# A dense layer with squared ReLU on one core: a new order of the first loads, and shared transposes for the tail columns of x

## The chip, the cores and the metric

The kernel runs on one core of a Trainium2 chip. The metric is the device time of one execution in microseconds; before the change three executions gave 290.81, 291.29 and 291.22, median 291.22. The profiled execution took 290.52, of which the profile's span is 288.7.

## What is computed

x is 2048 rows of D = 576 in bf16, w1 is 576 x 4608, w2 is 4608 x 576:

```python
h = jnp.einsum("bsd,df->bsf", x, w1) + b1
r = jnp.where(h > zero, h, zero)
h = r * r
out = jnp.einsum("bsf,fd->bsd", h, w2) + b2
```

576 is four and a half times 128. The half, the last 64 columns of x and the last 64 rows of w1, is what makes the layout below uneven.

## The kernel before, in words

The rows are worked in four token blocks of 512 (SB). For each block the kernel needs x transposed, with the 576 contraction values on the partitions. For blocks 1 to 3 the DMA transposes on the way in (load_xT). For block 0, x is loaded as it lies (load_x, line 71, four tiles of 128 rows, 144 KB each) and turned on TensorE, against an identity matrix, into PSUM, and copied from there to SBUF.

The transposed block, xT, has nine windows of 512 columns on 128 partitions, since the kernel uses TensorE in two ways. The first four of 36 feature tiles (G = 4) are computed with full 128-row matmuls: four chunks of 128 contraction rows, w1n, and a last 64-row piece, w1n8, for which two tiles go side by side, one on the upper and one on the lower 64 rows of the array (pair, lines 195 to 199). The other 32 feature tiles are computed in a row-split loop (a_rows, line 172): nine chunks of 64 rows each, one feature tile on partitions 0 to 63 and one on 64 to 127 at the same time. For this each half needs chunks that the transposes put on the other half, so two copies (dup_windows, line 113) duplicate four windows from one half of the partitions to the other. In names: windows O to O+3 are the four full chunks, E3 and SPC hold the tail and its neighbour, E to E+2 the shifted ones.

Each feature tile's PSUM bank is emptied by ScalarE (relu with bias, line 169) and squared by VectorE (line 170). After two blocks, phase_t and phase_b multiply by w2 and add b2, and then the other two blocks follow.

The order of the work is written by hand: keep() holds instructions in program order on each engine, and every engine works through its own stream. Loads are issued from SyncE and from ScalarE, each of which has a queue of its own. A load that reuses one of the eight completion semaphores waits until the earlier transfer on it has landed.

The head of the kernel, which the change concerns, is this:

- Seven matmuls on constants (WARM, line 61) keep TensorE busy until x arrives.
- SyncE issues x tiles 0 and 2, w1n chunks 0 and 2, the two halves of w1n8, and then the weights of the row-split loop (line 82). ScalarE issues x tiles 1 and 3 and w1n chunks 1 and 3, then loads its activation table with a small activation (line 97), and then issues b1 (line 98).
- Each x tile takes five transposes (x_transpose, line 141): four full chunks and the last 128 columns (D - P to D). So the tail transpose covers 64 columns that are in chunk 3 already. After two tiles the PSUM banks are copied (x_copies, line 148), by VectorE for three windows and by ScalarE for two. dup_windows(0) comes after the second half.
- The first four feature tiles are then summed chunk by chunk over half blocks of 256 columns (part(h, k), line 214), with the bias's transpose (make_b1T, line 157) in between, and finished by the pairs.

Of the kernel before, what the change touches and what calls it, by code (L numbers as in the profile page):

```python
# [9 lines left out]
ACT = mybir.ActivationFunctionType  # L10
ALU = mybir.AluOpType
BF16 = mybir.dt.bfloat16
FP32 = mybir.dt.float32
# [4 lines left out]
def kernel(  # L18
# [9 lines left out]
    nc = tc.nc  # L28
    keep = tc.keep_in_program_order
    P = 128  # L30
    H = 64
    x2 = x.flatten_outer_dims()
    out2 = out.flatten_outer_dims()
    S, D = x2.shape
    F = w1.shape[1]
    NFT = F // P
    NC = D // H
    NK = NC // 2
# [6 lines left out]
    RT = SB // P  # L45
# [3 lines left out]
    const = ctx.enter_context(tc.tile_pool(name="const", bufs=1))  # L49
# [6 lines left out]
    ps_h = ctx.enter_context(tc.tile_pool(name="ps_h", bufs=4, space=PSUM))  # L56
# [1 line left out]

    wps = ps_h.tile([P, 512], FP32, name="wps", tag="ph")
    ones = nc.const_aps.tensor(1.0, [P, 512], BF16)  # L60
    WARM = [512] * 6 + [256]
    for i, n in enumerate(WARM):
        keep(nc.tensor.matmul(wps[:, 0:n], lhsT=ones[:, 0:P], rhs=ones[:, 0:n], start=True, stop=True))  # L63

    xs = const.tile([P, RT, D], BF16, name="x_sb")
    w1n = wpool.tile([P, NK, GW], BF16, name="w1n")
# [4 lines left out]
    def load_x(eng, rt):  # L71
        keep(eng.dma_start(out=xs[:, rt, :], in_=x2[rt * P:(rt + 1) * P, :]))  # L72

    def load_w1n(eng, k0, k1):
        src = w1[k0 * P:k1 * P, 0:GW].rearrange("(k p) f -> p k f", p=P)
        keep(eng.dma_start(out=w1n[:, k0:k1, :], in_=src))

    def load_w1n8(eng, h):
        keep(eng.dma_start(out=w1n8[h * H:(h + 1) * H, :], in_=w1[NK * P:D, 0:GW]))
# [5 lines left out]
    b1_rows = const.tile([P, P], BF16, name="b1_rows")  # L85
    nc.vector.memset(b1_rows[:], 0.0)
    load_x(nc.sync, 0)
    load_x(nc.scalar, 1)
    load_x(nc.sync, 2)
    load_x(nc.scalar, 3)  # L90
    for k in range(NK):
        load_w1n(nc.sync if k % 2 == 0 else nc.scalar, k, k + 1)

    ident = const.tile([P, P], BF16, name="ident")
    make_identity(nc, ident[:])
    warm = const.tile([P, 1], FP32, name="warm")
    keep(nc.scalar.activation(out=warm[:], in_=nc.const_aps.tensor(0.0, [P, 1], FP32), func=ACT.Relu))
    keep(nc.scalar.dma_start(out=b1_rows[0:NFT, :], in_=b1.rearrange("(ft p) -> ft p", p=P)))
    for h in range(2):
        load_w1n8(nc.sync, h)  # L100

    E3, O, SPC, E = 0, 1, 5, 6
    LO_W = [O, O + 1, O + 2, O + 3, E, E + 1, E + 2, E3, SPC]
# [9 lines left out]
    def dup_windows(sb):  # L113
        xT = xT_blk[sb]
        keep(nc.vector.tensor_copy(out=xT[0:H, SPC:SPC + 4, :], in_=xT[H:P, E3:E3 + 4, :]))  # L115
        keep(nc.vector.tensor_copy(out=xT[H:P, SPC:SPC + 4, :], in_=xT[0:H, O:O + 4, :]))  # L116
# [18 lines left out]
    xT0 = xT_blk[0]  # L135
    HS = SB // 2
    tb = [[ps_h.tile([P, 4, HS], BF16, name="tb", tag="ph") for _ in range(2)] for _ in range(2)]
    PLACE = [(0, 0), (0, 1), (1, 0), (1, 1), (0, 2)]
    T_ORDER = [0, 1, NK, 2, 3]

    def x_transpose(j):
        h, q = divmod(j, 2)
        for k in T_ORDER:
            bank, slot = PLACE[k]
            c0 = k * P if k < NK else D - P
            keep(nc.tensor.transpose(tb[h][bank][:, slot, q * P:(q + 1) * P], xs[:, j, c0:c0 + P], ident[:]))

    def x_copies(h):
        hc = slice(h * HS, (h + 1) * HS)
        for k in (0, 1):  # L150
            keep(nc.vector.tensor_copy(out=xT0[:, O + k, hc], in_=tb[h][0][:, k, :]))
        keep(nc.scalar.copy(out=xT0[:, O + 2:O + 4, hc], in_=tb[h][1][:, 0:2, :]))  # L152
        keep(nc.vector.tensor_copy(out=xT0[:, E3, hc], in_=tb[h][0][:, 2, :]))

    b1T = const.tile([P, NFT], FP32, name="b1T")

    def make_b1T():
        b1T_ps = ps_h.tile([P, P], BF16, name="b1T_ps", tag="ph")
        keep(nc.tensor.transpose(b1T_ps[:], b1_rows[:], ident[:]))  # L159
        keep(nc.vector.tensor_copy(out=b1T[:], in_=b1T_ps[:, 0:NFT]))  # L160
# [6 lines left out]
    def evac_h(sb, bank, ft):  # L167
        r = rpool.tile([P, SB], BF16, name="r", tag="r")
        keep(nc.scalar.activation(out=r[:], in_=bank[:], func=ACT.Relu, bias=b1T[:, ft:ft + 1], scale=1.0))  # L169
        keep(nc.vector.tensor_tensor(out=hTs[sb][:, ft, :], in0=r[:], in1=r[:], op=ALU.mult))  # L170
# [17 lines left out]
    def a_full(sb, order):  # L188
        xT = xT_blk[sb]
        banks = []  # L190
        for g in range(G):
            pool, tag = (ps_o, "po") if g < 2 or order == "k_outer" else (ps_h, "ph")
            banks.append(pool.tile([P, SB], FP32, name="pn", tag=tag))

        def pair(i, start, stop):
            keep(nc.tensor.matmul(banks[2 * i][:], lhsT=w1n8[0:H, 2 * i * P:(2 * i + 1) * P], rhs=xT[0:H, SPC, :],  # L196
                             start=start, stop=stop, skip_group_check=order == "k_outer"))
            keep(nc.tensor.matmul(banks[2 * i + 1][:], lhsT=w1n8[H:P, (2 * i + 1) * P:(2 * i + 2) * P], rhs=xT[H:P, E3, :],  # L198
                             start=start, stop=stop, skip_group_check=order == "k_outer"))

        def full(g, k, start, stop):
            keep(nc.tensor.matmul(banks[g][:], lhsT=w1n[:, k, g * P:(g + 1) * P], rhs=xT[:, O + k, :],  # L202
                             start=start, stop=stop))

        if order == "rows_first":
            for i in (1, 0):
                pair(i, True, False)
            for g in (2, 3, 0, 1):
                for k in range(NK):
                    full(g, k, False, k == NK - 1)  # L210
                evac_h(sb, banks[g], g)
        else:
            if order == "k_outer":
                def part(h, k):
                    hc = slice(h * HS, (h + 1) * HS)
                    for g in range(G):
                        keep(nc.tensor.matmul(banks[g][:, hc], lhsT=w1n[:, k, g * P:(g + 1) * P],  # L217
                                              rhs=xT[:, O + k, hc], start=(h == 0 and k == 0), stop=False,
                                              skip_group_check=True))

                for j in range(2):
                    x_transpose(j)
                x_copies(0)
                for j in range(2, RT):
                    x_transpose(j)
                x_copies(1)
                dup_windows(0)
                for k in range(NK):
                    part(0, k)
                part(1, 0)  # L230
                make_b1T()
                for k in range(1, NK):
                    part(1, k)
            else:
                for g in (2, 3, 0, 1):
                    for k in range(NK):
                        full(g, k, k == 0, False)
            for i in (1, 0):
                pair(i, False, True)
                evac_h(sb, banks[2 * i], 2 * i)  # L240
                evac_h(sb, banks[2 * i + 1], 2 * i + 1)
# [42 lines left out]
    b2_col = const.tile([P, 1], BF16, name="b2_col")  # L284
    keep(nc.sync.dma_start(out=b2_col[:], in_=b2[DM:D].rearrange("(d o) -> d o", o=1)))
    b2T = const.tile([P, 1], FP32, name="b2T")
    nc.gpsimd.tensor_copy(out=b2T[:], in_=b2_col[:])
    keep(nc.sync.dma_start(out=b2_bc[:], in_=b2.partition_broadcast(P)))
    for c in range(2):
        load_w2(c)  # L290
# [1 line left out]

    alloc_hT(0)
    a_full(0, "k_outer")
    a_rows(0, 12, 1)
    alloc_hT(1)
    load_xT(3)
    a_rows(1)
    a_full(1, "rows_first")
    phase_t(0, hTs[0])  # L300
    phase_t(1, hTs[1])
    phase_b(0, hTs[0], dups=(2, 3))
    phase_b(1, hTs[1])
    alloc_hT(2)
    a_full(2, "g_outer")
    a_rows(2)
    alloc_hT(3)
# [36 lines left out]
```

## Time and profile before

| what | number |
|---|---|
| median of three executions | 291.22 us |
| span of the profile | 288.7 us |
| TensorE busy | 284.6 us, 99% |
| ScalarE, VectorE busy | 96.5, 78.6 us |
| row-split matmuls, lines 181 and 183 | 576 each, mean 376 ns |
| part, line 217 | 32 matmuls of 256 columns, first at 5.4 us |
| first pair, line 196 | 9.06 us |
| activation table load, line 97 | 1283 ns, at 2.61 us |

A busy TensorE in this profile is not a TensorE at its peak: matmuls are pipelined and their ends are modelled, so the start of one to the start of the next is the time that counts. The instructive part is the head: of its transfers the profile gives the issue and the time from issue to landing (x 2.8 to 3.2 us, w1n 3.5 to 3.9, w1n8 2.5 to 2.8).

### The profile page before, as it was taken

The numbers are of one execution on the slowest core, as the hardware profiler recorded it, in microseconds if no ns is written. First come the engines' busy times: TensorE is split into PE (matmuls) and PEld (weight loads), VectorE is DVE, ScalarE is ACT, GpSimd is POOL, SyncE is SP. The second block draws the span as 40 slices with busy tenths as digits, with TensorE's granted clock in tenths as the row PEclk, the third lists the DMA queues.
The fourth block names the chain that finished last, engine by engine and source line by source line (L and its number), as shares of the span: only waits on it lengthen the run. The fifth ranks groups of instructions, "written<-read, shape, count | busy, mean of one in ns | idle before, by whom it ended". The sixth has DMA issues, their size and how long they took to land.

```text
span 288.7 us, 4690 instructions
## 1 busy us (share of the span) xinstructions
PE 284.6 (99%) x2027; PEld 138.9 (48%) x2032; DVE 78.6 (27%) x177; ACT 96.5 (33%) x152; POOL 0.9 (0%) x7
## 2 busy tenths in 40 slices
PE   8999999999999999999999999999999999999996
PEld 5544444444444555555544444444444455555555
DVE  3444544444500200000025444444440001100001
ACT  3666666666500000000027666666670000000000
POOL 0000000000000000000000000000000000000000
PEclk9999999999999999999999999999999999999999
DMA  6999999600001100000000000000000110000000
GB/s 198 236 244 197 265 388 246 94 0 2 0 18 36 37 16 18 16 16 18 16 16 2 1 2 0 2 0 2 0 2 0 36 39 16 16 16 19 32 17 18
DMA packets 31573, 16.59 MB, mean 57 GB/s; under 512 B 15552, under 2 KB 31552, under 8 KB 31552
## 3 DMA queue, kind: packets, MB, share of 16 engines
q1 hardware_dynamic: 30928, 15.72, 22.3%
q10 hardware_dynamic: 624, 0.57, 0.7%
q8 instruction: 16, 0.26, 0.4%
q14 instruction: 5, 0.04, 0.0%
HBM read 11.43 MB, written 2.36 MB: 48 GB/s over the span
## 4 chain that ended last, share of the span: by engine, by line
PE 97%; DMA 1%; SPq 0%; issue 0%; DVE 0%
PE ph L181 42%; PE po L272 38%; PE pt L253 11%; PE pn L202 4%; DMA w1n<-in_w_dram 1%; PE pn L217 1%; PE ph L183 1%; PE pn L196 1%; SPq L72 0%; DVE o_sb L274 0%; PE b1T_ps L159 0%; PE pn L198 0%
## 5 line engine op out<-in xcount | busy, mean ns | idle before, releaser
L181 PE MATMUL ph<-xTw,w_h 64*128 64x512 bf16 x576 | 124.6, 376 | 0.0
L183 PE MATMUL ph<-xTw,w_h 64*128 64x512 bf16 x576 | 124.6, 376 | 0.0
L272 PE MATMUL po<-w_sb,hT 128*128 128x448 bf16 (+2 forms) x612 | 109.4, 341 | 0.0
L169 ACT ACTIVATE r<-ph,b1T 128x512 bf16<-128x512 f32 x128 | 81.1, 685 | 41.6 <-PE ph L183 41.6
L181 PEld LDWEIGHTS <-w_h 64*128 64x128 bf16 x576 | 54.1, 94 | 68.3
L272 PEld LDWEIGHTS <-hT 128*128 128x128 bf16 x612 | 58.5, 98 | 51.0
L170 DVE TENSOR_TENSOR hT<-r 128x512 bf16<-128x512 bf16 x144 | 61.2, 426 | 76.9 <-ACT r L169 76.9
L183 PEld LDWEIGHTS <-w_h 64*128 64x128 bf16 x576 | 54.1, 94 | 0.0
L274 DVE TENSOR_TENSOR o_sb<-po,b_bc 128x448 bf16<-128x448 f32 (+2 forms) x17 | 10.2, 597 | 125.8 <-PE po L272 125.8
L253 PE MATMUL pt<-hT,w_sb 128*128 128x512 bf16 x142 | 31.3, 379 | 0.1
L169 ACT ACTIVATE r<-pn,b1T 128x512 bf16<-128x512 f32 x16 | 10.3, 688 | 62.0 <-PE pn L198 60.6
L253 PEld LDWEIGHTS <-w_sb 128*128 128x128 bf16 x144 | 14.1, 98 | 17.0
L256 ACT ACTIVATE oT<-pt,b2T 128x512 bf16<-128x512 f32 x4 | 2.7, 687 | 28.3 <-PE pt L253 28.3
L202 PE MATMUL pn<-xTw,w1n 128*128 128x512 bf16 x45 | 10.4, 379 | 0.4 <-issue 0.3
L202 PEld LDWEIGHTS <-w1n 128*128 128x128 bf16 x48 | 4.5, 98 | 6.0 <-issue 0.8
L217 PE MATMUL pn<-xTw,w1n 128*128 128x256 bf16 x32 | 3.7, 273 | 0.1
L63 PE MATMUL wps<-const-bfloat16-1.0 128*128 128x512 bf16 (+1 forms) x7 | 2.9, 597 | 0.8 <-PEq L328 0.8
L217 PEld LDWEIGHTS <-w1n 128*128 128x128 bf16 x32 | 3.0, 98 | 0.6 <-DMA w1n<-in_w_dram 0.3
L115 DVE COPY xTw<-xTw 64x2048 bf16<-64x2048 bf16 x4 | 2.8, 690 | 0.6 <-ACT xTw L152 0.5
L116 DVE COPY xTw<-xTw 64x2048 bf16<-64x2048 bf16 x4 | 2.8, 688 | 0.1
L196 PE MATMUL pn<-xTw,w1n 64*128 64x512 bf16 x8 | 2.4, 379 | 0.0
L198 PE MATMUL pn<-xTw,w1n 64*128 64x512 bf16 x8 | 2.4, 379 | 0.0
(21 smaller groups left out, 10.5 us busy)
## 6 DMA issues: line engine op xcount, KB each, us to landing
w_sb<-in_w_dram SPq DMA_DIRECT2D x2, 2592.0 KB, 15.2
w_h<-in_w_dram SPq DMA_DIRECT2D x14, 288.0 KB, 6.6
out_dram<-o_sb SPq DMA_DIRECT2D x15, 112.0 KB, 1.7
w_h<-in_w_dram SPq DMA_DIRECT2D x4, 144.0 KB, 3.2
out_dram<-ot SPq DMA_DIRECT2D x4, 128.0 KB, 2.0
x_sb<-in_x_dram ACTq DMA_DIRECT2D x2, 144.0 KB, 3.0
x_sb<-in_x_dram SPq DMA_DIRECT2D x2, 144.0 KB, 3.0
w1n<-in_w_dram ACTq DMA_DIRECT2D x2, 128.0 KB, 3.6
```

The costliest lines, as they stand in the source:

```text
L63: keep(nc.tensor.matmul(wps[:, 0:n], lhsT=ones[:, 0:P], rhs=ones[:, 0:n], start=True, stop=True))
L115: keep(nc.vector.tensor_copy(out=xT[0:H, SPC:SPC + 4, :], in_=xT[H:P, E3:E3 + 4, :]))
L169: keep(nc.scalar.activation(out=r[:], in_=bank[:], func=ACT.Relu, bias=b1T[:, ft:ft + 1], scale=1.0))
L170: keep(nc.vector.tensor_tensor(out=hTs[sb][:, ft, :], in0=r[:], in1=r[:], op=ALU.mult))
L181: keep(nc.tensor.matmul(bx[:], lhsT=w1_h[0:H, LO_C[i], jc], rhs=xT[0:H, LO_W[i], :], start=(i == 0), stop=(i == NC - 1)))
L183: keep(nc.tensor.matmul(by[:], lhsT=w1_h[H:P, UP_C[i], jc], rhs=xT[H:P, UP_W[i], :], start=(i == 0), stop=(i == NC - 1)))
L196: keep(nc.tensor.matmul(banks[2 * i][:], lhsT=w1n8[0:H, 2 * i * P:(2 * i + 1) * P], rhs=xT[0:H, SPC, :], start=start, stop=stop, skip_grou ...
L202: keep(nc.tensor.matmul(banks[g][:], lhsT=w1n[:, k, g * P:(g + 1) * P], rhs=xT[:, O + k, :], start=start, stop=stop))
L217: keep(nc.tensor.matmul(banks[g][:, hc], lhsT=w1n[:, k, g * P:(g + 1) * P], rhs=xT[:, O + k, hc], start=(h == 0 and k == 0), stop=False, s ...
L253: keep(nc.tensor.matmul(pt[:], lhsT=w2_sb[:, ft, DM:D], rhs=hT[:, ft, :], start=(i == 0), stop=(i == NFT - 1)))
L272: keep(nc.tensor.matmul(po[:, 0:d1 - d0], lhsT=hT[:, ft, jj * P:(jj + 1) * P], rhs=w2_sb[:, ft, d0:d1], start=(i == 0), stop=(i == NFT - 1)))
L274: keep(nc.vector.tensor_tensor(out=o_sb[:, d0:d1], in0=po[:, 0:d1 - d0], in1=b2_bc[:, d0:d1], op=ALU.add))
```

## The change

It reorders the loads of the head. All four x tiles go on SyncE's queue, one after the other. ScalarE starts with the table load, whose small activation now writes one column of w1n chunk 0; the load of that chunk overwrites the column, so it is issued after the activation. Then ScalarE issues b1, chunks 0 and 2, and both halves of w1n8; SyncE has chunks 1 and 3.

The tail columns are no longer transposed with each tile. GpSimd gathers the 64 tail columns of two x tiles side by side (xs8), and one transpose turns both, so four tail transposes become two; they stand between the second and third part. The copies that spread their halves to E3 and SPC, and one shifted copy of four windows, are on VectorE. The shifted copy of three windows to the lower half goes to ScalarE (dup_windows_first). ScalarE copies two windows of the second half block only, where it copied two of each half. The warm-up is 384 columns shorter. The aim is an earlier first tile of x, less work on TensorE before the first matmuls, and less on VectorE.

```diff
-    WARM = [512] * 6 + [256]
+    WARM = [512] * 5 + [384]
...
     load_x(nc.sync, 0)
-    load_x(nc.scalar, 1)
-    load_x(nc.sync, 2)
-    load_x(nc.scalar, 3)
+    keep(nc.scalar.activation(out=w1n[:, 0, 0:1], in_=nc.const_aps.tensor(0.0, [P, 1], FP32), func=ACT.Relu))
+    keep(nc.scalar.dma_start(out=b1_rows[0:NFT, :], in_=b1.rearrange("(ft p) -> ft p", p=P)))
+    for rt in range(1, RT):
+        load_x(nc.sync, rt)
     for k in range(NK):
-        load_w1n(nc.sync if k % 2 == 0 else nc.scalar, k, k + 1)
+        load_w1n(nc.scalar if k % 2 == 0 else nc.sync, k, k + 1)
+    for h in range(2):
+        load_w1n8(nc.scalar, h)
...
-    warm = const.tile([P, 1], FP32, name="warm")
-    keep(nc.scalar.activation(out=warm[:], in_=nc.const_aps.tensor(0.0, [P, 1], FP32), func=ACT.Relu))
-    keep(nc.scalar.dma_start(out=b1_rows[0:NFT, :], in_=b1.rearrange("(ft p) -> ft p", p=P)))
+    xs8 = const.tile([P, RT, H], BF16, name="xs8")
     for h in range(2):
-        load_w1n8(nc.sync, h)
+        keep(nc.gpsimd.tensor_copy(out=xs8[:, 2 * h:2 * h + 2, :], in_=xs[:, 2 * h:2 * h + 2, NK * P:D]))
...
     def x_transpose(j):
         h, q = divmod(j, 2)
-        for k in T_ORDER:
-            bank, slot = PLACE[k]
-            c0 = k * P if k < NK else D - P
-            keep(nc.tensor.transpose(tb[h][bank][:, slot, q * P:(q + 1) * P], xs[:, j, c0:c0 + P], ident[:]))
-
-    def x_copies(h):
         hc = slice(h * HS, (h + 1) * HS)
-        for k in (0, 1):
-            keep(nc.vector.tensor_copy(out=xT0[:, O + k, hc], in_=tb[h][0][:, k, :]))
-        keep(nc.scalar.copy(out=xT0[:, O + 2:O + 4, hc], in_=tb[h][1][:, 0:2, :]))
-        keep(nc.vector.tensor_copy(out=xT0[:, E3, hc], in_=tb[h][0][:, 2, :]))
+        for bank in range(2):
+            for k in range(2 * bank, 2 * bank + 2):
+                keep(nc.tensor.transpose(tb[h][bank][:, k % 2, q * P:(q + 1) * P], xs[:, j, k * P:(k + 1) * P], ident[:]))
+            for k in range(2 * bank, 2 * bank + 2) if q == 1 else ():
+                copy = nc.scalar.copy if h == 1 and bank == 1 else nc.vector.tensor_copy
+                keep(copy(out=xT0[:, O + k, hc], in_=tb[h][bank][:, k % 2, :]))
...
+    def dup_windows_first():
+        keep(nc.scalar.copy(out=xT0[0:H, E:E + 3, :], in_=xT0[H:P, O:O + 3, :]))
+
+    def transpose_tails():
+        tl = ps_h.tile([P, 2, P], BF16, name="tl", tag="ph")
+        for h in range(2):
+            keep(nc.tensor.transpose(tl[:, h, :], xs8[:, 2 * h:2 * h + 2, :], ident[:]))
+        x8 = xT0.rearrange("p c (h q t) -> p c h q t", h=2, q=2)
+        for q in range(2):
+            keep(nc.vector.tensor_copy(out=x8[H:P, E3, :, q, :], in_=tl[q * H:(q + 1) * H, 0:2, :]))
+        for q in range(2):
+            keep(nc.vector.tensor_copy(out=x8[0:H, SPC, :, q, :], in_=tl[q * H:(q + 1) * H, 0:2, :]))
+        keep(nc.vector.tensor_copy(out=xT0[H:P, SPC:SPC + 4, :], in_=xT0[0:H, O:O + 4, :]))
+        keep(nc.vector.tensor_copy(out=xT0[0:H, E3, :], in_=xT0[H:P, O + 3, :]))
...
-                for j in range(2):
+                for j in range(RT):
                     x_transpose(j)
-                x_copies(0)
-                for j in range(2, RT):
-                    x_transpose(j)
-                x_copies(1)
-                dup_windows(0)
+                dup_windows_first()
+                part(0, 0)
+                part(0, 1)
+                transpose_tails()
+                part(0, 2)
+                part(0, 3)
                 for k in range(NK):
-                    part(0, k)
-                part(1, 0)
-                make_b1T()
-                for k in range(1, NK):
                     part(1, k)
+                    if k == 1:
+                        make_b1T()
```

The last edit of the diff fixes the place of a small GpSimd cast (b2T) in that engine's stream.

More of the change, by code (lines that the diff above doesn't have):

```diff
@@ L137 @@
     tb = [[ps_h.tile([P, 4, HS], BF16, name="tb", tag="ph") for _ in range(2)] for _ in range(2)]
-    PLACE = [(0, 0), (0, 1), (1, 0), (1, 1), (0, 2)]
-    T_ORDER = [0, 1, NK, 2, 3]
     def x_transpose(j):
         h, q = divmod(j, 2)
-        for k in T_ORDER:
-            bank, slot = PLACE[k]
-            c0 = k * P if k < NK else D - P
-            keep(nc.tensor.transpose(tb[h][bank][:, slot, q * P:(q + 1) * P], xs[:, j, c0:c0 + P], ident[:]))
-    def x_copies(h):
-        hc = slice(h * HS, (h + 1) * HS)
-        for k in (0, 1):
-            keep(nc.vector.tensor_copy(out=xT0[:, O + k, hc], in_=tb[h][0][:, k, :]))
-        keep(nc.scalar.copy(out=xT0[:, O + 2:O + 4, hc], in_=tb[h][1][:, 0:2, :]))
-        keep(nc.vector.tensor_copy(out=xT0[:, E3, hc], in_=tb[h][0][:, 2, :]))
-    b1T = const.tile([P, NFT], FP32, name="b1T")
+        hc = slice(h * HS, (h + 1) * HS)
+        for bank in range(2):
[4 more added lines that the diff above has]
+                keep(copy(out=xT0[:, O + k, hc], in_=tb[h][bank][:, k % 2, :]))
+    b1T = const.tile([P, NFT], FP32, name="b1T")
+    def dup_windows_first():
[11 more added lines that the diff above has]
+        keep(nc.vector.tensor_copy(out=xT0[0:H, E3, :], in_=xT0[H:P, O + 3, :]))
     def make_b1T():
@@ L286 @@
     b2T = const.tile([P, 1], FP32, name="b2T")
-    nc.gpsimd.tensor_copy(out=b2T[:], in_=b2_col[:])
+    keep(nc.gpsimd.tensor_copy(out=b2T[:], in_=b2_col[:]))
     keep(nc.sync.dma_start(out=b2_bc[:], in_=b2.partition_broadcast(P)))
```

## The prediction

> **What bounds the kernel now.** I read the page's busy table first, then the chain that ended last, then the same chain cut to the first ten microseconds.
>
> ```profile
> PE 284.6 (99%) x2027; PEld 138.9 (48%) x2032; DVE 78.6 (27%) x177; ACT 96.5 (33%) x152; POOL 0.9 (0%) x7
> ...
> PE 97%; DMA 1%; SPq 0%; issue 0%; DVE 0%
> ```
>
> TensorE is the bound of the whole span. The diff changes nothing in the streams after the first token block's first four feature tiles, so from the first pair of line 196 to the end the kernel must take what it takes now. The question is only when TensorE reaches that pair. The chain of the head says what sets it:
>
> ```profile
> 1.68 3.68 DMA w1n<-in_w_dram
> 5.36 0.05 issue
> 5.41 2.36 PE pn L217 x20
> 7.76 0.06 PE b1T_ps L159
> 7.82 1.31 PE pn L217 x12
> 9.13 0.32 PE pn L196
> ```
>
> w1 chunk 0, issued at 1.68 us, lands 3.68 us later; then TensorE never waits again. What ends just before is seen in the timeline of the weight loads:
>
> ```profile
> 2.86 0.15 PEld L63 LDWEIGHTS <-const-bfloat16-1.0 128*128 128x128 bf16 x1 [0.28 <-issue]
> 3.76 0.56 PEld L146 LDWEIGHTS <-x_sb 128*128 128x128 bf16 x10 [0.75 <-DMA x_sb<-in_x_dram]
> 4.55 0.56 PEld L146 LDWEIGHTS <-x_sb 128*128 128x128 bf16 x10 [0.23 <-DMA x_sb<-in_x_dram]
> 5.40 2.08 PEld L217 LDWEIGHTS <-w1n 128*128 128x128 bf16 x20 [0.29 <-DMA w1n<-in_w_dram]
> ...
> 9.06 0.09 PEld L196 LDWEIGHTS <-w1n 64*128 64x128 bf16 x1 [0.21 <-issue]
> ```
>
> Two waits for x, then one for w1 chunk 0. The last x tile was in at 4.55 and its transposes were through by about 5.11 (ten at 0.056): x is 0.29 us off the path, w1 chunk 0 is on it. The table of stretches shows that the transfers are the cause (columns: window, length, busy of PE, PEld, DVE, ACT, POOL, clock, DMA share, GB/s):
>
> ```profile
> 1.00:1.50 0.50, 0.50 (x2) 0.15 (x1) 0.00 (x0) 0.00 (x0) 0.29 (x1) 1.00 0.00 0
> 1.50:2.00 0.50, 0.50 (x2) 0.15 (x1) 0.00 (x0) 0.00 (x0) 0.00 (x0) 1.00 0.38 83
> 2.00:2.50 0.50, 0.50 (x3) 0.22 (x2) 0.00 (x0) 0.00 (x0) 0.00 (x0) 1.00 1.00 247
> ...
> 4.50:5.00 0.50, 0.45 (x8) 0.45 (x9) 0.50 (x3) 0.00 (x0) 0.00 (x0) 1.00 1.09 379
> ```
>
> Data starts to flow some 1.15 us after the first issue (0.73), and the engines are then full, at 250 to 380 GB/s, until the w1 chunks are in.
>
> **What the Trainium skill says.** "DMA: Bandwidth & Descriptors", section "Issuing engines are not separate DMA queues": transfers issued from several engines run on the same 16 DMA engines and interleave; a second queue only saves issue time. The trace agrees: two x tiles issued at 0.73, one per queue, landed together after 3.0 and 2.8 us. So one queue for x brings order, not bandwidth. "ScalarE: Activation LUTs", section "What ACT_TABLE_LOAD costs": about 1283 ns; the trace has 1283 ns at line 97. "TensorE: Matmul & The Clock Gate", section "What's actually happening": the array runs at half rate until a free-running window of about 3.4 us has been busy. The trace agrees that it begins slow: warm-up weight loads stand 0.43 us apart (2.44, 2.86) for 512 columns, later matmuls 0.215.
>
> **The change, part by part.**
>
> *w1 chunk 0 (the path).* Now it is issued at 1.68 but queued behind x. In the new order ScalarE first does the table load (0.73 + 1.28 = 2.01), the small activation (0.20, to 2.23 with gaps) and the b1 issue (0.70 by its row at line 98, to 2.95), so chunk 0 is issued at 3.00: 1.32 us later. By then SyncE has issued x at about 0.73, 1.20, 1.68 and 2.16 (pitch 0.46 to 0.48), chunk 1 at 2.62 and, after x tile 0 is in, chunk 3 near 3.1. Data of chunk 0 starts at 3.00 + 1.15 = 4.15, when x is nearly through (last issue 2.16 + 1.15 + 147 KB at 313 GB/s, 0.47 = 3.8). Chunk 0 then shares the engines with chunks 1 and 3: 131 KB at half of some 330 GB/s, 0.8 us, to 4.95. From the end of data to the semaphore, the old x pair gives 0.5 us (295 KB from 1.9 at 310 GB/s end at 2.85 to 2.95, landing 3.5 at the earlier). Landing: 5.45. Bounds: alone on the engines it takes 1.15 + 0.4 + 0.5 = 2.05 us, landing at 5.05; like the old first x pair (2.8), 5.8. I take 5.45, against 5.36 now: **+0.09**.
>
> *x in order, transposes 20 to 16 before the first matmuls.* x tile 0 shares with nobody, so it lands about 0.5 us earlier than 3.72, the last near 4.4 (now 4.5). Four transposes after that take 0.22, to 4.65, even at half rate 4.85. Hidden behind chunk 0 either way: 0.
>
> *Warm-up 3328 columns to 2944.* 384 columns at the slow pitch (0.43 per 512) are 0.32 us, of TensorE time before x is in: the warm-up ends near 3.25 instead of 3.55. 0, as long as the clock has risen by 5.45.
>
> *Tail transposes.* Two at 0.056 between parts (0,1) and (0,2): **+0.11** on TensorE's path. They wait for GpSimd's gather of 128 elements. The nearest rows are its 128x128 ops at 0.20 and 0.29; the page "GPSIMD Engine Reference", section 3.1, gives 2.6 cycles an element, estimated 0.28 plus dispatch, so I bound it by 0.2 and 0.7. After the last x (4.4) it is done by 5.2 at worst; the transposes come at 5.45 + 8 x 0.109 = 6.3. Hidden.
>
> *Copies.* ScalarE now issues two more transfers (0.58 each, the line 79 row), and the second waits for the b1 landing, near 4.3; so it is free at about 5.2, copies 128x256 twice (under 0.59 each, the 512-wide row) to 6.3 at worst, and then the 64x1536 shifted copy. From 202 ns for 1 element and 588 for 512, that is 0.20 + 1535 x 0.755 = 1.36 us: done by 7.7. Its readers are the fifth pair of the row-split loop, after 9.9, and queued behind it are only the relu evictions, which now start at 9.48. VectorE: tail transposes end near 6.6, four 64x256 copies from PSUM (0.28 each, the 128x256 row; pitch 0.2) to 7.7, the 64x2048 copy (0.69) to 8.4, the 64x512 copy (0.2 to 0.3) to 8.7, b1T (0.2) to 8.9. The first pair, at 9.2, needs only the tail copies; the row-split loop needs the rest from 9.65 on; the first eviction needs b1T at 9.6. Slack is 0.7 us or more: hidden.
>
> *Queue of the row-split weights.* SyncE no longer issues the two 64-row chunks (1.21 us) and starts line 82's loads when x tile 2 has landed, near 3.9 instead of 4.79. They land no later than now: 0.
>
> *Sum.* Chunk 0 at 5.45 (+0.09) and two transposes (+0.11) on TensorE: first pair at 9.06 + 0.20 = 9.26, and with rounding of the waits 0.1 to 0.2 us late. 291.22 + 0.1 = 291.3.
>
> **The rivals.**
>
> *A, likeliest: the wait moves but keeps its place, 291.3.* Anything of chunk 0 between 4.9 and 5.9 belongs here, that is -0.4 to +0.6 us.
>
> *B, faster: the transfers answer quicker when x and w1 don't mix, 290.6.* For it: the 112 KB stores of the output take 1.7 us from issue to landing with nothing beside them. Chunk 0 would land at 4.7, just as the x transposes end, and the first pair would come at 4.7 + 3.65 (now 9.06 - 5.41) + 0.11 = 8.46, 0.6 earlier. Against it: no load of 128 KB or more did better than 2.8 us here, and chunk 2, issued near 3.5, would then be the next wait. The x part could add to it, if runs without a profile wait longer for x than this one.
>
> *C, slower: the clock or the chunk comes late, 292.2.* The warm-up is 0.32 us shorter and the transposes come in four little groups with gaps, then TensorE idles from 4.65 to 5.45. In this trace the pitch is slow up to the last warm-up matmul (3.29) and 0.056 for the transposes at 3.76, so the clock rose between. If that window now fails and the next, 3.4 us on (near 7.1), raises it, the matmuls from 5.45 to 7.1 run at half rate and lose 0.8 us; with +0.2, about 292.2. A chunk 0 landing at 6.0 or later gives the same side. Against it: 2.5 of 3.4 us is still busy before x arrives, and x now arrives as the warm-up ends.
>
> **How the numbers follow.** A 0.48, B 0.28, C 0.24. One measurement's 0.2% is 0.58 us, so A is "within", B "faster", C "slower". The predicted time is A's, 291.3. The range: B's 290.6 with the lower end of the executions before (290.81 against the median 291.22, 0.4) gives 290.3, and C's gives 292.2; about 2 in 10 stay outside, mostly a clock that rises later still.
>
> **What would show it.** Right: in the new trace the first line 227 weight load waits for w1n, near 5.4 to 5.5, and the first pair follows 3.75 us later; x tile 0's transposes start near 3.2; no wait for Pool or VectorE between. Wrong: matmuls of 256 columns 0.21 apart after 5.5 (C); chunk 0 in at 4.7 and the wait gone to x (B); a wait ahead of the pairs for VectorE's copies or of the row-split loop for w_h, which I cost at nothing.

## The result, and the profile after

The changed kernel takes 292.72 us in the median of six executions (291.48 to 292.88), the kernel before 291.12 in the same comparison; the ratio is 1.0046, 95% interval 1.0025 to 1.0067. It is slower, and the time lies above the predicted range (290.3 to 292.2). The six executions stand apart in two groups, two at 291.5 to 291.7 and four at 292.7 to 292.9. The profile shown first is of the lower group (291.48).

The chain that ended last, cut to the head of the changed kernel (start, length, what):

```profile
2.60 3.82 DMA w1n<-in_w_dram
6.42 0.05 issue
6.47 0.61 PE pn L227 x4
7.08 0.11 PE tl L158 x2
7.19 1.75 PE pn L227 x16
8.94 0.06 PE b1T_ps L169
9.00 0.87 PE pn L227 x8
9.87 0.32 PE pn L206
```

In this trace, too, a w1 chunk leads the chain, but it is chunk 1, issued at 2.60 us behind x on SyncE's queue, and not chunk 0. The timeline of the weight loads of the same run:

```profile
2.86 0.15 PEld L145 LDWEIGHTS <-x_sb 128*128 128x128 bf16 x1 [0.28 <-DMA x_sb<-in_x_dram]
3.18 0.36 PEld L145 LDWEIGHTS <-x_sb 128*128 128x128 bf16 x3 [0.17 <-issue]
4.08 0.77 PEld L145 LDWEIGHTS <-x_sb 128*128 128x128 bf16 x8 [0.54 <-DMA x_sb<-in_x_dram]
5.09 0.34 PEld L145 LDWEIGHTS <-x_sb 128*128 128x128 bf16 x4 [0.24 <-DMA x_sb<-in_x_dram]
5.39 0.61 PEld L227 LDWEIGHTS <-w1n 128*128 128x128 bf16 x4
6.47 0.33 PEld L227 LDWEIGHTS <-w1n 128*128 128x128 bf16 x4 [0.47 <-DMA w1n<-in_w_dram]
...
9.80 0.09 PEld L206 LDWEIGHTS <-w1n 64*128 64x128 bf16 x1 [0.21 <-issue]
```

x tile 0 is in early, as meant (landed at 2.81, before 3.72). But tile 3 is late: its transposes start at 5.09, where the old kernel's last transposes started at 4.55 as a group of ten. The first pair comes at 9.80 instead of 9.06. The starts of the matmuls split these 0.74 us: 0.09 for the first short part (5.50 instead of 5.41); 0.19 for two short parts that ran at 0.21 and 0.19 us instead of 0.109; 0.35 waiting for chunk 1; 0.11 for the two tail transposes.

The span grew by 0.96 us (288.7 to 289.7; the trace of before is of a quick execution, 290.52 us), so 0.22 more lies behind the head. The groups of the weight loads between 30 and 36 us show it (line, count, busy, mean ns, idle before and what ended it):

```profile
L191 PEld LDWEIGHTS <-w_h 64*128 64x128 bf16 x28 | 2.6, 94 | 1.7
L193 PEld LDWEIGHTS <-w_h 64*128 64x128 bf16 x27 | 2.5, 94 | 1.5 <-DMA w_h<-in_w_dram 0.3
```

TensorE waits 0.33 us for row-split weights, which it never did in the trace of before. Their stream is slower from early on. The table of stretches for 10 to 20 us, the kernel before first (the last two columns are the share of the DMA engines and GB/s):

```profile
10.00:20.00 10.00, 10.00 (x96) 4.51 (x94) 5.11 (x12) 7.45 (x13) 0.00 (x0) 1.00 1.21 256
```

and the changed kernel:

```profile
10.00:20.00 10.00, 10.00 (x96) 4.90 (x94) 5.11 (x12) 7.37 (x12) 0.00 (x0) 1.00 1.23 200
```

The engines are as busy and move a fifth less. In the trace's records of DMA packets, the 512-byte packets of w_h have a median of 36 ns before and 47 after.

### The profile page after: what moved, and what is told of

It reads as the page before. It is cut to its first block, busy times and chain, and to the rows that moved or that the text cites. A ratio compares the mean times of both kernels' runs of the same rounds, so it can differ in the third digit from the quotient of the medians.

```text
span 289.7 us, 4695 instructions
## 1 busy us (share of the span) xinstructions
PE 285.3 (98%) x2024; PEld 140.6 (49%) x2029; DVE 79.3 (27%) x181; ACT 97.4 (34%) x153; POOL 1.5 (1%) x9
## 4 chain that ended last, share of the span: by engine, by line
PE 97%; DMA 1%; SPq 1%; issue 0%; DVE 0%
PE po L281 38%; PE ph L191 29%; PE ph L193 14%; PE pt L262 11%; PE pn L212 4%; DMA w1n<-in_w_dram 1%; PE pn L227 1%; SPq L72 1%; PE pn L206 1%; PE pn L208 0%; DVE o_sb L283 0%; PE tl L158 0%; PE b1T_ps L169 0%
## 5 line engine op out<-in xcount | busy, mean ns | idle before, releaser
L145 PE MATMUL tb<-ident,x_sb 128*128 128x128 bf16 x16 | 2.2, 310 | 0.3 <-DMA x_sb<-in_x_dram 0.3
L148 DVE COPY xTw<-tb 128x256 bf16<-128x256 bf16 x6 | 1.4, 285 | 3.7 <-PE tb L145 3.6
```

## The experiments

Two things were to be explained: what slows the changed kernel in general, and what parts the two groups. Three theories came up. The **order** theory: one queue for x brings the last tiles and chunk 1 late. The **clock** theory, rival C of the prediction: the array stays at half rate for longer. And the **address** theory. The change drops a tile of 4 bytes (warm), which took up 32, and adds one of 512 (xs8), so every tile allocated behind them starts 480 bytes later: w1_h at 28640 instead of 28160, which is 55 times 512. In the new place it stands 224 bytes past a multiple of 256. w1n and the weights w2_sb move by the same 480 bytes.

In the first four expectations below, theory 1 is the order and the clock together; theory 2 is the slow stream of w_h, still without a cause.

All medians in one table; the kernel before, measured beside them on each chip, had 290.94 to 290.99.

| run | chip | median us (executions) | ratio, 95% interval | at 292.5 or more |
|---|---|---|---|---|
| after_again | 1 | 291.52 (6) | 1.0015 to 1.0039 | 0 |
| long_warm_restored | 1 | 291.67 (9) | 1.0022 to 1.0053 | 1 |
| old_loads | 1 | 290.99 (22) | 0.9999 to 1.0013 | 0 |
| before_short_warm | 1 | 291.02 (22) | 0.9999 to 1.0014 | 0 |
| after_realigned | 13 | 291.67 (22) | 1.0022 to 1.0053 | 9 |
| before_shifted | 13 | 291.70 (19) | 1.0015 to 1.0033 | 2 |
| before_new_loads | 13 | 291.08 (13) | 0.9995 to 1.0016 | 0 |
| chunk1_on_scalar | 13 | 291.67 (16) | 1.0017 to 1.0053 | 7 |
| realigned_long_warm | 7 | 291.24 (13) | 1.0004 to 1.0028 | 1 |
| before_three_warm | 7 | 291.81 (14) | 1.0017 to 1.0040 | 2 |
| before_shifted_64 | 7 | 291.47 (18) | 1.0010 to 1.0024 | 0 |
| before_shifted_128 | 4 | 291.31 (13) | 1.0000 to 1.0016 | 0 |
| before_shifted_256 | 4 | 290.83 (13) | 0.9989 to 1.0004 | 0 |
| early_start | 7 | 291.28 (21) | 1.0003 to 1.0016 | 0 |
| after_third | 4 | 293.30 (6) | 1.0052 to 1.0086 | 4 |
| after_fourth | 4 | 292.68 (7) | 1.0026 to 1.0057 | 4 |

### One part at a time

**after_again**: no edit.

> The changed kernel unaltered, for a second trace of it and a paired time. Theory 1 (two waits in the head: w1 chunk 1 behind x in one queue, and a TensorE clock that rises late because the warm-up is shorter): first pair of line 206 at 9.8 us or later, the time 291.5 to 292.9; where the time is near 292.8 the short parts of line 227 stand 0.21 us apart past 7 us. Theory 2 (the row-split weights stream more slowly and TensorE waits for w_h later on): the first pair again near 9.8 and the rest, up to 2 us, in waits of lines 191 and 193 for w_h.

291.29 to 291.77, all in the lower group. The first pair came at 9.53, and near 33 us TensorE waited for w_h again. So both theories had a part of it, and the upper group isn't in every set of executions: on this chip it didn't appear.

**long_warm_restored**:

```diff
-    WARM = [512] * 5 + [384]
+    WARM = [512] * 6 + [256]
```

> The changed kernel with the old warm-up of 3328 columns, nothing else. Theory 1: the clock rises as it did before, at 3.7 us, the executions near 292.8 vanish, and what remains is the wait for chunk 1: first pair near 9.6, median 291.5 to 291.8. Theory 2 (w_h): no difference to the changed kernel, median 292.7.

291.67 is within what was expected, but so was the unaltered kernel on that chip, so it decides nothing on the clock: its own trace shows no early rise either. One of nine was at 293.26.

**old_loads**, the changed kernel with the loads of before:

```diff
-    keep(nc.scalar.activation(out=w1n[:, 0, 0:1], ...))
-    ...            # x on SyncE, b1, chunks 0 and 2, w1n8 on ScalarE
+    load_x(nc.sync, 0)
+    load_x(nc.scalar, 1)
+    load_x(nc.sync, 2)
+    load_x(nc.scalar, 3)
+    for k in range(NK):
+        load_w1n(nc.sync if k % 2 == 0 else nc.scalar, k, k + 1)
...
+    warm = const.tile([P, 1], FP32, name="warm")
```

> The changed kernel with the loads of the kernel before (x on two queues, chunks 0 and 2 on SyncE, 1 and 3 on ScalarE, table load after them, w1n8 on SyncE), keeping the short warm-up and the shared tail transposes. Theory 1: the wait for chunk 1 is gone, the first parts follow each other; the clock may still rise late, so 291.1 with the clock early and up to 292.3 with it late. Theory 2, if the new order is what slows w_h: no wait for w_h any more, median 291.2.

290.99, no slower than before. So the shared tail transposes, the ScalarE copy and the short warm-up together cost nothing that can be measured here (the interval ends at 0.13%), and all of the loss that after_again shows on this chip goes with this edit. But the edit undoes two things at once: the order, and with the warm tile the addresses.

**before_short_warm**, the WARM line of the change in the kernel before.

> The kernel before with the short warm-up of 2944 columns, nothing else. Theory 1: the clock loses its early window in most executions, and the median is 0.5 to 1.2 us above the kernel before, 291.6 to 292.3. Theory 2 and every theory in which the warm-up doesn't matter: 291.1, no difference.

291.02. Theory 1 expected at least 291.6: it fell. With the old loads the short warm-up cost nothing on this chip. As to the upper group, this run and old_loads say less than their 44 executions promise, because the unaltered changed kernel had none there on this chip either.

The trace is of one of the slower executions (291.74). A line of its list of waits (in all, times, longest, in us):

```profile
PEld L183 <- DMA w_h<-in_w_dram: 1.3, 2, 0.7
```

This kernel has the old addresses and packets of 36 ns, and yet TensorE waits for w_h. So such a wait in one trace isn't a mark of the slow stream.

### Addresses against order

**after_realigned**, an unused tile of 32 bytes in the dropped one's place:

```diff
+    pad = const.tile([P, 8], FP32, name="pad")
     ident = const.tile([P, P], BF16, name="ident")
```

> The changed kernel with an unused 32-byte tile in place of the tile that the change dropped, so that w1n, the row-split weights, w2 and the later tiles begin at multiples of 64 bytes in SBUF again (they stand at 32 beyond one in the changed kernel). Address theory: the 512-byte packets of w_h take 36 ns in the middle again (48 in the changed kernel), no wait of TensorE for w_h near 33 us, and the median falls from 291.5 to 291.0 to 291.2; what is left is the late chunk 1. Order theory (the new order alone costs all of it, the slow stream follows from it): packets stay at 48 ns, median 291.5.

w_h packets have a median of 38 ns. The trace has no wait for w_h, but it is of an upper execution, in which TensorE comes to these weights later. The lower executions profiled with realigned tiles (chunk1_on_scalar, realigned_long_warm) have none either. Of 22 executions 13 form a lower group with a median of 291.28, where the lower group of the changed kernel (13 of 25 executions over four runs) has 291.62. So about 0.34 us of the lower group is the address; the two runs with the long warm-up, long_warm_restored and realigned_long_warm, differ by 0.43 in the median. (These runs were on different chips, on which the kernel before differs by 0.05 at most.) The whole median stayed at 291.67, because nine executions are at 292.7 and above: there the address isn't the cause.

**before_shifted**, the same line in the kernel before, where it does the opposite.

> The kernel before with an unused 32-byte tile more, so that the same tiles begin 32 bytes beyond a multiple of 64. Nothing else differs. Address theory: w_h packets at 48 ns instead of 36, a stream of 200 GB/s instead of 260 between 10 and 20 us, waits of 0.3 us or more for w_h, median 0.2 to 0.6 us above the kernel before. Order theory: no difference, 36 ns.

291.70, 0.24% slower, w_h packets at 47 ns. The stretch from 10 to 20 us:

```profile
10.00:20.00 10.00, 9.92 (x92) 4.29 (x89) 5.09 (x12) 7.37 (x12) 0.00 (x0) 1.00 1.18 203
```

and the groups of weight loads from 13 to 15 us of the same run:

```profile
L184 PEld LDWEIGHTS <-w_h 64*128 64x128 bf16 x7 | 0.6, 94 | 0.8 <-DMA w_h<-in_w_dram 0.6
```

One unused tile slows the stream from 256 to 203 GB/s and adds 0.7 us to the median: that the addresses cost time is shown. By which waits is shown less well. A wait for w_h stands in the trace of before_short_warm too, and here TensorE also waits longer in the head (the longest 0.98 us, where before had 0.29):

```profile
PEld L218 <- DMA w1n<-in_w_dram: 1.3, 2, 1.0
```

w1n, w1_h and w2_sb all moved, and no run moved one of them alone. The packets of w1n (1024 bytes) have a median of 46 ns in both traces, so this wait isn't explained by them.

**before_new_loads**, the kernel before with the new order of loads, addresses kept by the pad tile:

```diff
-    load_x(nc.scalar, 1)
-    load_x(nc.sync, 2)
-    load_x(nc.scalar, 3)
+    keep(nc.scalar.activation(out=w1n[:, 0, 0:1], ...))
+    ...            # as in the change
+    pad = const.tile([P, 8], FP32, name="pad")
```

> The kernel before with the new order of the loads alone (x on SyncE's queue, the activation into chunk 0, b1, chunks 0 and 2 and w1n8 on ScalarE's), with the 32-byte tile that keeps the addresses at multiples of 64. Order theory: x tile 3 lands after 5.0 us instead of 4.5 and chunk 1 after 6.1, first pair 0.4 to 0.7 later than 9.06, median 291.4 to 291.6. Address theory alone: no difference, 290.9 to 291.1.

291.08: not 291.4 to 291.6. The order theory as I had put it fell. Its trace shows the lateness well, in one of the slower of its executions:

```profile
4.68 0.28 PEld L145 LDWEIGHTS <-x_sb 128*128 128x128 bf16 x5 [0.47 <-DMA x_sb<-in_x_dram]
6.45 0.28 PEld L145 LDWEIGHTS <-x_sb 128*128 128x128 bf16 x5 [1.49 <-DMA x_sb<-in_x_dram]
```

x tile 3 comes after a wait of 1.49 us, and yet the median moves by 0.1 us, which isn't clear of zero. What one queue costs on average is small when the warm-up is long.

**chunk1_on_scalar**, chunk 1 moved out from behind x, realigned:

```diff
-        load_w1n(nc.scalar if k % 2 == 0 else nc.sync, k, k + 1)
+        load_w1n(nc.scalar if k < 2 else nc.sync, k, k + 1)
```

> The realigned changed kernel with chunks 0 and 1 on ScalarE's queue and 2 and 3 behind x on SyncE's, so that chunk 1 no longer stands behind x. If the wait for chunk 1 in SyncE's queue is what costs in the head, it lands near 5.7 instead of 6.2 to 6.4, the second group of short parts follows the first, and the median is 0.3 to 0.5 us below that of the realigned kernel. If x tile 3 (after 5.0 us) is the limit by itself, the median moves by less than 0.2 us.

291.67, the lower group at 291.28, both as in the realigned kernel. But the edit didn't bring chunk 1 earlier. The weight loads of its trace:

```profile
5.89 0.23 PEld L146 LDWEIGHTS <-x_sb 128*128 128x128 bf16 x4 [1.05 <-DMA x_sb<-in_x_dram]
6.12 0.35 PEld L228 LDWEIGHTS <-w1n 128*128 128x128 bf16 x4
7.03 0.22 PEld L228 LDWEIGHTS <-w1n 128*128 128x128 bf16 x3 [0.56 <-DMA w1n<-in_w_dram]
```

The second group of w1n loads is chunk 1's, and TensorE waits for it here too: issued at 2.66 on ScalarE's queue, it landed at 6.99, where behind x it had landed at 6.42. So its place behind x isn't shown to be what makes it late, and what the wait for it costs stays open. x tile 3, weight loads at 5.89, is late besides.

### The upper group

after_realigned gave a profile of an upper execution by chance, span 293.1 us (at 294.88 us the slowest of its 22): its short parts stood 0.213 us apart from 6.95 to 12.07. The next runs test that.

**realigned_long_warm**, the pad tile and the old WARM line.

> The realigned changed kernel with the old warm-up of 3328 columns. Clock theory: the realigned kernel had two groups of executions, 291.0 to 291.4 and 292.6 to 293.2, the upper one with a TensorE clock that stays slow until about 12 us, because a short warm-up is followed by waits for single x tiles. With the longer warm-up at most 1 in 10 is in the upper group, and the median is 291.1 to 291.3. If the upper group has another cause (the transfers), a third or more of the executions stays above 292.5.

One of 13 at 293.23, the median 291.24. With the short warm-up, the realigned kernel had 9 of 22 up there, and chunk1_on_scalar 7 of 16. That is what the clock theory expects, though on another chip.

**before_three_warm**:

```diff
-    WARM = [512] * 6 + [256]
+    WARM = [512] * 3
```

> The kernel before with a warm-up of 1536 columns (three matmuls), nothing else: loads, transposes and addresses are those of the kernel before. Clock theory: TensorE idles from 2.1 to 3.6 us, so the clock rises late in a third or more of the executions, which then take 292.0 to 293.5, while the rest stays at 291. Theory that the upper group belongs to the new loads: no execution above 292.2.

291.81 in the median, so a warm-up that ends 1.5 us ahead of x costs 0.3% with the old loads too. In its trace the parts stand 0.213 us apart until 8.3. The split into two groups that I expected isn't there: 2 of 14 are above 292.5, the others spread from 291.1 to 292.5.

**after_third** and **after_fourth**, no edit.

> The changed kernel unaltered, for more executions and another trace. Its executions so far fall into two groups, 291.3 to 291.8 and 292.7 to 292.9. Clock theory: a fifth to a half of the new ones is in the upper group; if the trace is of one of these, short parts stand 0.21 us apart well past 6 us. Transfer theory: in the upper group the parts are 0.11 apart and the time lies in waits for x, w1n or w_h.

> The same kernel once more: as for the one before it. Together they say how large the upper group is.

Eight of 13 in the upper group, 12 of 25 over all runs of this kernel (lower median 291.62, upper 292.84). The trace of after_fourth is of an upper one (292.74). The short parts alone in two stretches (columns: window, length, busy and count of PE and PEld, clock, DMA share, GB/s; the clock column is 1.00 even where the matmuls stand at half rate, so the counts have to tell):

```profile
6.40:8.40 2.00, 1.93 (x9) 1.24 (x10) 1.00 0.59 140
8.60:10.00 1.40, 1.40 (x14) 1.27 (x13) 1.00 1.05 222
```

Nine in 2.0 us (and two tail transposes), then fourteen in 1.4: the array runs at half rate until 8.6. In the same stretch of the lower execution shown first:

```profile
6.40:8.40 2.00, 1.93 (x17) 1.59 (x18) 1.00 1.05 213
```

The timeline of after_fourth says where the time goes before:

```profile
3.01 0.96 PEld L145 LDWEIGHTS <-x_sb 128*128 128x128 bf16 x8 [0.43 <-DMA x_sb<-in_x_dram]
5.32 0.35 PEld L145 LDWEIGHTS <-x_sb 128*128 128x128 bf16 x4 [1.35 <-DMA x_sb<-in_x_dram]
6.06 0.34 PEld L145 LDWEIGHTS <-x_sb 128*128 128x128 bf16 x4 [0.39 <-DMA x_sb<-in_x_dram]
6.39 0.65 PEld L227 LDWEIGHTS <-w1n 128*128 128x128 bf16 x4
```

TensorE idles for 1.35 us, does two more groups of transposes, and starts the first matmuls at 6.46, at half rate. The first pair comes at 11.28, 1.48 us after that of the lower execution: 0.96 from the later start, 0.9 from more work at half rate, less the 0.35 of waiting for chunk 1, which by then has landed. This is what the clock theory expects; a wait for w_h is absent here.

Is it the idling, then? The lower traces of the same kernel help. Each trace also records from when the full rate was granted: from 5.87 us in the lower execution shown first, 5.14 in after_again, 3.55 in after_third and 8.63 in after_fourth; the spacing of the matmuls changes at these times. The weight loads of after_again, and the last x tile of after_third:

```profile
2.99 0.98 PEld L145 LDWEIGHTS <-x_sb 128*128 128x128 bf16 x8 [0.41 <-DMA x_sb<-in_x_dram]
4.74 0.34 PEld L145 LDWEIGHTS <-x_sb 128*128 128x128 bf16 x4 [0.77 <-DMA x_sb<-in_x_dram]
```

```profile
5.70 0.23 PEld L145 LDWEIGHTS <-x_sb 128*128 128x128 bf16 x4 [1.28 <-DMA x_sb<-in_x_dram]
```

after_again and after_fourth run alike, within 0.01 us, up to their eighth transpose at 3.93. Then one idles 0.77 us and the rate rises at 5.14; the other idles 1.35, and the rate stays low for 3.49 us more. after_third idles about as long, 1.28 us, but its rate had risen at 3.55, stayed up, and the execution is in the lower group. So in these traces idling costs the rate when it comes before the rise. If the rate is decided window by window, 3.41 us each (below), a window of after_fourth ended at 8.63 - 3.41 = 5.22, close to after_again's 5.14. So these two hardly differ in when their windows lie, and differ in the idling. It is a comparison of single traces, not a test.

### How far an address may be off

**before_shifted_64**, **before_shifted_128**, **before_shifted_256**: the pad line with 16, 32 and 64 columns.

> The kernel before with an unused 64-byte tile more: w1n, w_h, w2 and the later tiles begin 64 bytes beyond a multiple of 512. If multiples of 64 are what counts, no difference: packets of 36 to 39 ns, median 291.0. If it is the multiple of 512 (or 128) that was lost with the 32-byte shift, packets at 47 to 48 ns and 291.5 to 291.8, as with the 32-byte shift.

> The kernel before with an unused 128-byte tile more, so that w_h and the tiles after it begin 128 bytes beyond a multiple of 512. If a multiple of 128 is enough: packets of 36 to 39 ns and 291.0. If not: 44 to 48 ns and 291.4 to 291.8, as with 32 and 64 bytes.

> The kernel before with an unused 256-byte tile more: the tiles begin 256 bytes beyond a multiple of 512. If a multiple of 256 is enough: 36 to 39 ns and 291.0. If only the multiple of 512 will do: 44 to 48 ns and 291.4 to 291.8.

| w1_h beyond a multiple of 512 | packet, median | GB/s, 10 to 20 us | median us |
|---|---|---|---|
| 0 | 36 ns | 256 | 290.97 |
| 32 | 47 | 203 | 291.70 |
| 64 | 44 | 212 | 291.47 |
| 128 | 42 | 224 | 291.31 |
| 256 | 35 | 254 | 290.83 |

Multiples of 64 and of 128 are not enough; a multiple of 256 is. The time of the median execution follows the packets. The changed kernel, 224 bytes beyond a multiple of 256, has 47 ns and 200 GB/s as at 32: what the two have in common is that they stand 32 bytes from the nearest multiple. The Trainium skill names the same boundary: "DMA: Bandwidth & Descriptors", section "How a descriptor splits into AXI transactions", says that the transactions a descriptor is cut into must start at multiples of 256 bytes, and that the bytes ahead of an odd start are fetched for nothing. By that rule 512 bytes off the boundary would need three transactions instead of two, an estimate. The boundary agrees with the table. The page speaks of bytes fetched, though, and here it is the destination in SBUF that is off; and its count of beats doesn't agree: estimated by it, 128 would cost more than 32, and the runs show the reverse. So the boundary is shown, and the mechanism is not.

### A version from the pieces

**early_start**: old queues, aligned tiles, old warm-up, shared tails, and chunks 0 and 1 ahead of x tiles 2 and 3, with the first two parts ahead of these tiles' transposes.

The loads, against those of the kernel before (shortened):

```diff
     load_x(nc.sync, 0)
     load_x(nc.scalar, 1)
+    load_w1n(nc.sync, 0, 1)
+    load_w1n(nc.scalar, 1, 2)
     load_x(nc.sync, 2)
     load_x(nc.scalar, 3)
+    load_w1n(nc.sync, 2, 3)
+    load_w1n(nc.scalar, 3, 4)
-    for k in range(NK):
-        ...
```

> A version from the pieces: loads on both queues as before, but chunks 0 and 1 ahead of x tiles 2 and 3; the old warm-up; aligned tiles; the shared tail transposes; the first half block's parts 0 and 1 before the transposes of x tiles 2 and 3. If the first 0.5 MB in the right order lets TensorE start earlier: first short part at 4.6 us instead of 5.4, first pair near 8.9 instead of 9.1 to 9.2, median 290.7 to 290.9. If the sum of the bytes is what counts, the first pair is where it was and the median 291.0.

291.28, slower than before by 0.10% (0.03 to 0.16). The first part starts at 4.55, as hoped, and then TensorE waits for what was pushed back:

```profile
4.55 0.75 PEld L231 LDWEIGHTS <-w1n 128*128 128x128 bf16 x7 [0.39 <-issue]
5.96 0.48 PEld L149 LDWEIGHTS <-x_sb 128*128 128x128 bf16 x8 [0.65 <-DMA x_sb<-in_x_dram]
6.71 0.33 PEld L231 LDWEIGHTS <-w1n 128*128 128x128 bf16 x4 [0.27 <-DMA w1n<-in_w_dram]
```

The first pair is at 9.60. No version of these runs beats the kernel before.

## Why the prediction was wrong

**"The diff changes nothing in the streams after the first token block's first four feature tiles, so from the first pair of line 196 to the end the kernel must take what it takes now."** This failed. The instructions are the same, but their operands lie elsewhere. That costs about 0.34 us in the lower group (after_realigned), and up to 0.7 where it is put into the kernel before. The same error stands in "They land no later than now: 0": w_h is issued earlier (4.44 instead of 4.79) and still comes too late at 33 us.

**"0, as long as the clock has risen by 5.45."** This step weighs most in the median of the six, four of which are in the upper group. The condition didn't hold. In the lower execution the parts run at full rate from about 5.9, in the upper ones until 8.6 or later not at all. I had this as rival C with a chance of 0.24 and 0.8 us; it is 12 of 25 executions and 1.2 us (291.62 to 292.84). Rival C had the kind of loss right and the place of the idling wrong: it put it after the transposes, from 4.65 to 5.45, where it waits for chunk 0; in the traces TensorE idles for single x tiles before. I argued that 2.5 of 3.4 us would still be busy. The Trainium skill's "TensorE: Matmul & The Clock Gate", section "What's actually happening", says that the window is free-running, so it may begin anywhere. From this I infer that a window that begins later than the warm-up's start sees less of it, and then the idling for x. The prediction took the phase of one trace as fixed. The traces agree with the length of 3.4 us that the prediction took from this page: the full rate lasts 286.72 us in nine of them and 283.31 in seven, 84 and 83 times 3.413 us. They show it begin anywhere between 3.6 and 8.6 us, and once near 12.5. In before_shifted_256, whose head is that of the kernel before, it begins at 5.64 instead of 3.66. That the window's phase, together with the idling, parts the groups stays an inference, since no run could set it.

**"Hidden behind chunk 0 either way: 0" (x in order).** The first tile came early as meant, and earlier than "about 0.5 us earlier than 3.72", that is 3.2: at 2.81 here, at 2.9 to 3.0 in the other traces with the new order. The last wasn't: 4.4 expected, 5.05 in this trace and 5.2 to 6.5 in the other traces with the new order, where old_loads has 4.64. Alone that is worth 0.1 us, within noise (before_new_loads). With the short warm-up it makes the idling in which the clock isn't raised: short warm-up and old order had no execution of 44 above 292, new order with the long warm-up 2 of 35 above 292.5 (realigned or not), both together 28 of 63. These counts mix chips. On chip 1, where the 44 ran, both together had none of 6 either. The one comparison on a single chip is before_new_loads, none of 13, beside after_realigned and chunk1_on_scalar, 16 of 38; the transposes differ there as well as the warm-up. So that it takes both is likely, and not shown.

**Chunk 0 at 5.45.** It came at 5.24 here, and at 5.5 to 6.7 in the other traces with the new order, each time within 0.3 us of x tile 3. It was issued at 2.26 and not 3.00, because ScalarE issued b1 at 0.96, while the table load was still running (0.73 to 2.01); I had put them end to end. That this term came out close is luck. The wait that I named wasn't the one: TensorE waited for x tile 3 and for chunk 1.

**Right:** two tail transposes, 0.11 in the chain. The gather on GpSimd, 0.29 each and done at 5.46, within its bounds. The copies: ScalarE's shifted one 1.47 us (1.36 expected) and done at 7.88, VectorE's last at 9.70 against the first eviction at 10.22, nobody waits for them. old_loads confirms these parts together at no measurable cost. (One slip: the range's lower end, 290.6 less 0.4, is 290.2 and not 290.3; nothing hangs on it.)

The sum for a typical execution, from the medians: 290.97 before; 0.1 for the order, a figure within noise; 0.2 for what is left in the realigned lower group (291.28), in which the two transposes are 0.11 and the rest isn't told apart; 0.34 for the addresses: 291.62. Half of the executions (12 of 25) add 1.2 for the clock.

## What to carry to other kernels

A diff that adds or drops a tile, however small and unused, moves every tile behind it: look at the addresses, and try the targets of wide loads at multiples of 256 bytes. A warm-up may be lost when TensorE idles between it and the first real work before the rate has risen: here a shorter warm-up and a later arrival of the data cost nothing clear of noise one at a time, and together 28 of 63 executions stood above 292.5. And a kernel whose executions fall into groups needs a trace from each group before a cause is named.

## What I had not expected

- 512-byte packets into SBUF rows that stand 32 bytes from a multiple of 256, on either side, had a median of 47 ns instead of 36, and less the further off (44 at 64 bytes, 42 at 128).
- ScalarE issues transfers while its activation table is being loaded: b1's issue began 0.23 us into the load of 1.28 us and took 0.62. Its packets moved from 2.18 us on, after the load.
- x on one queue was through later than on two: the last x packet ended at 4.7 to 5.9 us in the nine traces with one queue, and at 3.9 to 4.2 in the eight with two queues and x ahead of w1. So "order, not bandwidth" in the prediction fell short. A part of it is the issue, since tile 3 is issued at 2.13 instead of 1.20. Why the rest is open: no run here isolated a cause.
